# The output weights' bit conversion through a PSUM bank, and a new order of all steps

## The chip, the core and the metric

The program runs on one core of one Trainium2 chip. The metric is the device time of one execution in microseconds (us). Five engines work side by side: TensorE (PE, matmuls; PEld is its weight load), VectorE (DVE), ScalarE (ACT), GpSimd (POOL) and SyncE (SP), which here issues every DMA. PE, DVE and ACT write PSUM, a buffer of eight banks of 128 x 512 float32; all else lies in SBUF.

## What is computed

Three blocks follow each other on 8 batches of 576 rows of width 512. In short:

```python
# attention over pooled keys and values (8 heads of 64; pool of 8 along the sequence: 576 -> 72)
k_p, v_p = mean over 8 rows of k, v
x = softmax(q @ k_p.T / 8) @ v_p                      # (8, 576, 512)
# first MLP: 512 -> 1024 -> 512
h = relu(x @ w_in); c = conv over 3 neighbouring rows of h with conv_w
x = (h * sigmoid(c)) @ w_out                          # w_out: 1024 x 512
# second MLP with spatial gating
h = gelu(x @ w_in2); u, v = two halves of h; v = layernorm(v) * g_ln
out = x + (u * (w_sg @ v + b_sg)) @ w_out2            # w_out2: 512 x 512
```

Five inputs (`w_in`, `conv_w`, `w_out`, `w_in2`, `w_out2`) come as 64-bit floats, and the kernel turns them into float32 by bit operations.

## The kernel before

Matmuls run on operands that are split into a high part (rounded to the format fp32r) and a low remainder; a product is three matmuls, high x high, low x high and high x low.

**Tasks and steps.** Every piece of work is a generator. A step is what it issues between two `yield`s. A table of step keys, `ORDER`, names in one line of text which generator goes on next: a letter for the task, a number for its tile, and after the point the batch or chunk. Each instruction is pinned behind the one before it on its engine, so `ORDER` fixes the order on every engine, and that of SP's DMAs. The tasks that matter here:

- `k`, `v`, `q`/`p` load keys, values and queries; `K` makes the pooled, transposed keys `KBT` (for batch 1 by summing on PE, L106, then copies on ACT, L295/L296, and on DVE, L298/L301); `s` makes scores on PE (L419) and the softmax; `e` the transposed weights; `a` attention times values into `xh` and `xl`.
- `i` converts a piece of `w_in`, `t` a piece of `w_out` (8 of each), `l` a piece of `w_out2` (4).
- `I` is a tile of the first MLP's hidden layer: 12 matmuls into a bank `psi`, then relu and a tap on ACT (L558, L568), two taps on DVE (L570, L571), tanh on ACT (L573), and `g` on DVE (L577), which is the last reader of the bank. `O` multiplies by `w_out` into three banks `pso`; after the last tile ACT (L604) and DVE (L602) empty them.
- `y` loads the first MLP's result transposed, `T` makes the operands `xc` of the second MLP from it (subtractions on POOL, L694; high part on ACT, L699; low part on DVE or POOL, L134); `n` and `u` are its products (L747).
- `L`, `S`, `R` load and split the normalised half, `d` is the spatial product (L747, with evictions on DVE, L977, and the gate on POOL, L981), `D` splits the gated values, `o` multiplies by `w_out2` into a bank `psi` and stores.

**Banks.** PSUM's eight banks are three `psa`, two `psi` and three `pso`, each kind used in turn. A tile that asks for a bank waits for the last reader of the tile that had it before.

**A conversion.** `weight` loads 128 x 1024 words (512 KB), and `to_f32` makes 128 x 512 float32 of them by three DVE instructions: L146 writes an intermediate, L149 changes it in place, L152 writes `t`, a tile of the pool `work` with three buffers (tag `y`, shared with `g` and other short-lived tiles). ACT then rounds `t` to the high part and POOL (for `w_out2` DVE) subtracts. For `w_in` the intermediate lies in a bank `pso`; for `w_out` and `w_out2` it is `t` itself.

**Stages.** By the profile's time: attention of batch 0 and the first weights up to 63 us; attention of batch 1, the first tiles `I`/`O` and all of `t` up to 121 us; attention and first MLP together up to 554 us; second MLP's products up to 750 us; spatial product and output up to the end.

Of the kernel before, what the change touches and what calls it, by code (L numbers as in the profile page):

```python
# [26 lines left out]
def pooled_attention_gated_mlps(  # L27
# [24 lines left out]
    w_in, conv_w, w_out, w_in2, w_out2 = (a.bitcast(U32) for a in (w_in, conv_w, w_out, w_in2, w_out2))  # L52
    B, H, S, D = q.shape
# [26 lines left out]
    slot = ctx.enter_context(tc.tile_pool(name="slot", bufs=1))  # L80
# [27 lines left out]
    dve, pool = nc.vector, nc.gpsimd  # L108
    LO_IN = [pool for f in range(NF)]
    LO_OUT = [pool for f in range(NF)]  # L110
# [22 lines left out]
    def subtract(out, in0, hi, eng=nc.vector):  # L133
        eng.tensor_tensor(out=out, in0=in0, in1=hi.bitcast(F32), op=ALU.subtract)  # L134

    def to_f32(raw, t, tmp=None):

        w = raw.rearrange("p (n t) -> p t n", t=2)
        lo, up = w[:, 0, :], w[:, 1, :]
        ti = t.bitcast(U32)
        mi = ti if tmp is None else tmp.bitcast(U32)
        nc.vector.tensor_scalar(out=mi, in0=up, scalar1=3, scalar2=0x3FFFFFF8,  # L146
                                op0=ALU.logical_shift_left, op1=ALU.bitwise_and)
        yield
        nc.vector.scalar_tensor_tensor(out=mi, in0=up, scalar=0xC0000000, in1=mi,  # L149
                                       op0=ALU.bitwise_and, op1=ALU.bitwise_or)  # L150
        yield
        nc.vector.scalar_tensor_tensor(out=ti, in0=lo, scalar=29, in1=mi,  # L152
                                       op0=ALU.logical_shift_right, op1=ALU.bitwise_or)
        yield
# [43 lines left out]
    def weight(pool_, tag, src, eng, bank_, done):  # L198
        raw = pool_.tile([128, 1024], U32, tag=tag, name=f"{tag}raw")
        dst = raw  # L200
        if len(src.shape) == 3:
            dst = raw.rearrange("p (a b) -> p a b", a=src.shape[1])
        nc.sync.dma_start(out=dst, in_=src)
        yield
        t = work.tile([128, 512], F32, tag="y", name="t")
        yield from to_f32(raw, t, bank_() if bank_ else None)
        hl = pool_.tile([128, 2, 512], F32R, tag=tag, name=f"{tag}hl")
        done(hl)
        nc.scalar.copy(out=hl[:, 0, :], in_=t)
        yield  # L210
        subtract(hl[:, 1, :], t, hl[:, 0, :], eng)
# [11 lines left out]
    def t_w_out(f, *_):  # L223
        return weight(slot, f"w{f}", w_out[128 * f:128 * f + 128, :], LO_OUT[f], None,
                      lambda hl: wo.__setitem__(f, hl))
# [384 lines left out]
    w2 = {}  # L610
# [289 lines left out]
    wo2 = {}  # L900

    def t_w_out2(i, *_):
        p, tag = ((slot, "w4"), (slot, "w6"), (w2["q"], "T3"), (w2["q"], "T4"))[i]
        return weight(p, tag, w_out2[128 * i:128 * i + 128, :], dve, None, lambda hl: wo2.__setitem__(i, hl))
# [35 lines left out]
    g2 = {}  # L940
# [81 lines left out]
    def t_o2(i, b):  # L1022
# [14 lines left out]
        else:  # L1037
            for e in range(2):
                r0 = S * (b - 1 + e) + 128 * NM
                nc.sync.dma_start(out=out[r0:r0 + REM, :], in_=ob[REM * e:REM * e + REM])  # L1040


    tasks = {"z": t_setup, "c": t_coef, "i": t_w_in, "t": t_w_out, "k": t_k, "K": t_kfin, "v": t_v, "V": t_vfin,
             "q": t_q, "p": t_qtr, "s": t_s, "e": t_e, "x": t_x, "h": t_hg, "a": t_a, "I": t_i, "O": t_o, "A": t_att_close,
             "w": t_w2, "W": t_wsum, "Q": t_wsplit, "B": t_x2_open, "y": t_x2, "T": t_xc, "n": t_v2, "u": t_u,
             "g": t_sg, "G": t_sgsum, "H": t_sgsplit, "J": t_sgrest, "l": t_w_out2, "L": t_load, "S": t_sc, "R": t_vr,
             "b": t_bsg, "U": t_uload, "d": t_sp, "D": t_g, "m": t_res, "o": t_o2}
    running = {}
# [4 lines left out]
    def step(key):  # L1053

        if key not in running:
            i, _, b = key[1:].partition(".")
            running[key] = iter(tasks[key[0]](int(i or 0), int(b or 0)) or ())
        more = next(running[key], 0)
        issued = nc.cur_bb.bb.instructions
        for n in range(seen[0], len(issued)):  # L1060
            ins = issued[n]
            if ins.engine in last:
                tc.add_manual_dep(ins, last[ins.engine], pin, reason="order")
            last[ins.engine] = ins.name
        seen[0] = len(issued)
        return more is None

    for key in ORDER.split():
        step(key)
# [30 lines left out]
```

## Time and profile before

| | |
|---|---|
| median of 3 runs | 967.24 us (965.71 to 967.61) |
| the profiled execution's own time | 966.23 us |
| its span, first to last instruction | 964.3 us |
| mean granted clock of TensorE | 0.989 of full speed |
| busy PE / DVE / POOL / ACT | 923.4 / 776.4 / 562.8 / 529.3 us |

The span is what the views below show; 1.93 us of the execution's time lie around it. "Busy" of PE is not PE at its peak: a matmul that runs at half the clock is busy for longer. In a row of the timeline the first number is the start, the second the time until the end, and what stands in brackets is the engine's idle time before the row and what ended it.

### The profile page before, as it was taken

How to read it: one execution, taken by the hardware profiler on the slowest of the kernel's cores; microseconds unless marked ns; L12 is line 12 of the kernel's file. 1: busy time of each engine (PE TensorE's matmuls, PEld its weight loads, DVE VectorE, ACT ScalarE, POOL GpSimd, SP SyncE). 2: the span in 40 equal slices, each digit the busy share in tenths (PEclk: the TensorE clock that was granted, in tenths of full speed). 3: DMA queues.
4: the chain of work that ended last, by engine and by line, in shares of the span. 5: the costliest groups of instructions: out<-in, count | busy, mean ns of one | idle time of the engine just before them, and what ended most of it. 6: DMA issues, size and time to landing. Idle time of an engine off the chain costs nothing.

```text
span 964.3 us, 15821 instructions
## 1 busy us (share of the span) xinstructions
PE 923.4 (96%) x5396; PEld 844.2 (88%) x5396; DVE 776.4 (81%) x1399; ACT 529.3 (55%) x1108; POOL 562.8 (58%) x630
## 2 busy tenths in 40 slices
PE   5899999999999999999999989999999899999998
PEld 4787789899899998898998889999999788999996
DVE  5888997878889788797788478898887887887773
ACT  2756576667767666766557356655656323332221
POOL 3777797877868676356345257544563655554430
PEclk9899999999999999999999989999999999999999
DMA  9966174555747446232620674576536557476454
GB/s 241 243 190 164 45 186 118 131 148 155 158 129 145 129 126 138 60 104 69 157 70 22 123 150 119 156 204 171 146 140 217 179 156 259 142 219 180 159 179 131
DMA packets 182700, 143.61 MB, mean 149 GB/s; under 512 B 99776, under 2 KB 136924, under 8 KB 182620
## 3 DMA queue, kind: packets, MB, share of 16 engines
q1 hardware_dynamic: 182620, 142.61, 55.1%
q8 instruction: 42, 0.69, 0.3%
q14 instruction: 38, 0.31, 0.1%
HBM read 94.20 MB, written 48.37 MB: 148 GB/s over the span
## 4 chain that ended last, share of the span: by engine, by line
PE 75%; POOL 8%; DVE 8%; issue 3%; DMA 2%; ACT 2%; SPq 1%; POOLq 0%; DVEq 0%; ACTq 0%
PE psi L106 18%; PE psa L747 13%; PE pso L747 12%; PE pso L99 5%; PE pso L101 5%; PE pso L100 5%; PE psi L99 3%; PE psi L100 3%; PE psi L101 3%; PE psa L106 3%; PE psa L419 3%; POOL raw L251 1%; POOL xb L694 1%; POOL en L449 1%; DVE t L152 1%
## 5 line engine op out<-in xcount | busy, mean ns | idle before, releaser
L134 POOL TENSOR_TENSOR hg<-g,hg 128x384 fp32r<-128x384 f32 x96 | 100.3, 1053 | 74.2 <-ACT hg L580 68.0
L981 POOL TENSOR_TENSOR u<-u,tmp 128x288 f32<-128x288 f32 x64 | 60.6, 965 | 61.9 <-DVE tmp L977 41.6
L573 ACT ACTIVATE psi<-psi 128x384 f32<-128x384 f32 x96 | 45.7, 477 | 62.5 <-DVE psi L571 62.2
L694 POOL TENSOR_TENSOR xb<-xb 128x768 f32<-128x768 f32 x24 | 46.5, 1938 | 55.1 <-DVE xc L134 14.3
L570 DVE SCALAR_TENSOR_TENSOR psi<-h,coef,psi 128x384 f32<-128x384 f32 x96 | 58.7, 611 | 20.1 <-ACT psi L568 19.7
L558 ACT ACTIVATE h<-psi 128x386 f32<-128x386 f32 (+1 forms) x96 | 47.4, 493 | 43.5 <-PE psi L106 42.9
L617 ACT CAST sc<-vf 128x512 fp32r<-128x512 f32 x48 | 29.0, 620 | 72.6 <-POOL vf L928 42.2
L134 POOL TENSOR_TENSOR eTl<-xb,eTh 128x512 fp32r<-128x512 f32 (+1 forms) x30 | 46.4, 1545 | 32.9 <-ACT eTh L503 32.8
L577 DVE SCALAR_TENSOR_TENSOR g<-psi,h 128x384 f32<-128x384 f32 x96 | 52.5, 548 | 13.3 <-ACT psi L573 10.8
L571 DVE SCALAR_TENSOR_TENSOR psi<-h,coef,psi 128x384 f32<-128x384 f32 x96 | 59.8, 623 | 3.4
L419 PE MATMUL psa<-KBT,qT 128*128 128x144 f32 (+1 forms) x320 | 54.5, 300 | 7.5 <-DVE KBT L298 3.0
L419 PEld LDWEIGHTS psa<-KBT,qT 128*128 128x128 f32 (+1 forms) x320 | 45.6, 185 | 15.3 <-DVE KBT L298 3.3
L568 ACT ACTIVATE psi<-h,coef 128x384 f32<-128x384 f32 x96 | 56.3, 586 | 3.1
L747 PE MATMUL pso<-wc,xc 128*128 128x256 f32 x378 | 52.1, 286 | 6.0 <-ACT ob L604 2.9
L747 PEld LDWEIGHTS pso<-wc,xc 128*128 128x128 f32 x378 | 49.5, 192 | 7.4 <-ACT ob L604 3.3
L580 ACT CAST hg<-g 128x384 fp32r<-128x384 f32 x96 | 47.7, 507 | 14.3 <-DVE g L577 13.7
L747 PE MATMUL psa<-wc,xc 128*128 128x256 f32 x378 | 51.4, 283 | 1.1 <-ACT tmp L770 1.0
L747 PEld LDWEIGHTS psa<-wc,xc 128*128 128x128 f32 x378 | 49.0, 189 | 1.7 <-ACT tmp L770 1.4
L747 PE MATMUL psa<-xc,wc 128*128 128x384 f32 x252 | 49.7, 346 | 0.3 <-ACT tmp L814 0.2
L747 PE MATMUL pso<-xc,wc 128*128 128x384 f32 x252 | 49.1, 338 | 0.6 <-ACT tmp L814 0.6
L699 ACT CAST xc<-xb 128x768 fp32r<-128x768 f32 x42 | 34.6, 835 | 23.1 <-DVE xb L682 11.9
L457 POOL TENSOR_TENSOR en<-e,rs 128x512 f32<-128x512 f32 (+1 forms) x30 | 32.0, 1066 | 24.4 <-ACT hg L580 10.1
(396 smaller groups left out, 3120.2 us busy)
## 6 DMA issues: line engine op xcount, KB each, us to landing
xb<-eds SPq DMA_DIRECT2D x24, 384.0 KB, 3.4
x2s<-ob SPq DMA_DIRECT2D x36, 256.0 KB, 2.3
xb<-x2s SPq DMA_DIRECT2D x48, 192.0 KB, 4.1
us<-ub SPq DMA_DIRECT2D x24, 384.0 KB, 3.2
vs<-vg SPq DMA_DIRECT2D x18, 512.0 KB, 3.2
u<-us SPq DMA_DIRECT2D x16, 576.0 KB, 6.2
vf<-vs SPq DMA_DIRECT2D x16, 512.0 KB, 4.5
out_dram<-ob SPq DMA_DIRECT2D x32, 256.0 KB, 2.0
```

The source lines that it names most:

```text
L99: nc.tensor.matmul(out=out_, lhsT=ah, rhs=bh, start=first, stop=False)
L100: nc.tensor.matmul(out=out_, lhsT=al, rhs=bh, start=False, stop=False)
L101: nc.tensor.matmul(out=out_, lhsT=ah, rhs=bl, start=False, stop=last)
L106: nc.tensor.matmul(out=out_, lhsT=a, rhs=b_, start=(i == 0), stop=(i == n - 1))
L134: eng.tensor_tensor(out=out, in0=in0, in1=hi.bitcast(F32), op=ALU.subtract)
L419: nc.tensor.matmul(out=ps[0:n, 2 * SP * x:2 * SP * x + 2 * SP], lhsT=qT[:, p, 0:n], rhs=KBT[:, p, :], start=True, stop=True)
L568: nc.scalar.activation(out=y, in_=tap(1), func=AF.Copy, scale=cw(1, f))
L570: nc.vector.scalar_tensor_tensor(out=y, in0=tap(0), scalar=cw(0, f), in1=y, op0=ALU.mult, op1=ALU.add)
L571: nc.vector.scalar_tensor_tensor(out=y, in0=tap(2), scalar=cw(2, f), in1=y, op0=ALU.mult, op1=ALU.add)
L694: pool.tensor_tensor(out=x, in0=y, in1=z, op=ALU.subtract)
L747: nc.tensor.matmul(out=ps, lhsT=a, rhs=b_, start=first and i == 0, stop=last and i == n - 1, skip_group_check=True)
L981: pool.tensor_tensor(out=z, in0=z, in1=o, op=ALU.mult)
```

## The change

The two tasks give `weight` a bank of the kind `psi` for the intermediate, so that L146 and L149 write PSUM and only L152 writes SBUF. And `ORDER` is another line of text: the same 3617 steps, each as often as before, in a different sequence.

```diff
-ORDER = '''z k0.0 k1.0 k2.0 z z p0.0 c p1.0 p2.0 v0.0 v1.0 p3.0 ...'''
+ORDER = '''(the same keys in another sequence)'''
...
     def t_w_out(f, *_):
-        return weight(slot, f"w{f}", w_out[128 * f:128 * f + 128, :], LO_OUT[f], None,
+        return weight(slot, f"w{f}", w_out[128 * f:128 * f + 128, :], LO_OUT[f], i_bank,
                       lambda hl: wo.__setitem__(f, hl))
...
-        return weight(p, tag, w_out2[128 * i:128 * i + 128, :], dve, None, lambda hl: wo2.__setitem__(i, hl))
+        return weight(p, tag, w_out2[128 * i:128 * i + 128, :], dve, i_bank, lambda hl: wo2.__setitem__(i, hl))
```

DVE, around the first conversion of `w_out` (`w0raw`) and the pooled keys of batch 1 (`KBT`); `psi<-h,coef,psi` are the taps of the first tile `I`, `g` its end. Before:

```order
L146 TENSOR_SCALAR t<-w0raw 128x512
L149 SCALAR_TENSOR_TENSOR t<-w0raw,t 128x512
L152 SCALAR_TENSOR_TENSOR t<-w0raw,t 128x512
L570 SCALAR_TENSOR_TENSOR psi<-h,coef,psi 128x384
L571 SCALAR_TENSOR_TENSOR psi<-h,coef,psi 128x384
L298 COPY KBT<-psa 64x3x72
L301 COPY KBT<-psa 64x64
L146 TENSOR_SCALAR t<-w1raw 128x512
L149 SCALAR_TENSOR_TENSOR t<-w1raw,t 128x512
L577 SCALAR_TENSOR_TENSOR g<-psi,h 128x384
L152 SCALAR_TENSOR_TENSOR t<-w1raw,t 128x512
```

The same place now:

```order
L146 TENSOR_SCALAR psi<-w0raw 128x512
L149 SCALAR_TENSOR_TENSOR psi<-w0raw,psi 128x512
L570 SCALAR_TENSOR_TENSOR psi<-h,coef,psi 128x384
L571 SCALAR_TENSOR_TENSOR psi<-h,coef,psi 128x384
L152 SCALAR_TENSOR_TENSOR t<-w0raw,psi 128x512
L577 SCALAR_TENSOR_TENSOR g<-psi,h 128x384
L298 COPY KBT<-psa 64x3x72
L301 COPY KBT<-psa 64x64
L146 TENSOR_SCALAR psi<-w1raw 128x512
L149 SCALAR_TENSOR_TENSOR psi<-w1raw,psi 128x512
L152 SCALAR_TENSOR_TENSOR t<-w1raw,psi 128x512
```

The two conversions have no other work between their last instructions and the copies of `KBT`: the copies now stand behind `g`, and the second conversion is whole behind them.

PE at the same place: 40 sums of batch 1's keys (`ident,st`), the first tile `I` (`wi0hl`), transposes of queries (`ident,qb`, L397) and the scores (L419) that read `KBT`. Before:

```order
L106 MATMUL psa<-ident,st_174 64x128 x24
L106 MATMUL psi<-xh,wi0hl 128x386
...
L106 MATMUL psa<-ident,st_174 64x128 x8
L106 MATMUL psa<-ident,st_174 64x64 x8
L419 MATMUL psa<-KBT,qT 128x144 x2
L106 MATMUL psi<-xh,wi1hl 128x386
```

Now:

```order
L106 MATMUL psa<-ident,st_174 64x128 x16
L106 MATMUL psi<-xh,wi0hl 128x386
...
L106 MATMUL psa<-ident,st_174 64x128 x16
L106 MATMUL psa<-ident,st_174 64x64 x8
L397 MATMUL psa<-ident,qb 128x128 x4
L419 MATMUL psa<-KBT,qT 128x144 x4
L106 MATMUL psi<-xh,wi1hl 128x386
```

The tile `I` stands 8 sums further ahead, four transposes stand between the last sums and the scores, and both halves of the scores come before the next tile `I`.

ACT, where the first MLP ends and the second begins: `xc<-xb` are the high parts of the new operands (L699), `ob<-pso` empties the banks of the last `O`. Before:

```order
L580 CAST hg<-g 128x384 x2
L699 CAST xc<-xb 128x768 x4
L604 ACTIVATE ob<-pso 128x512
L699 CAST xc<-xb 128x768
L604 ACTIVATE ob<-pso 128x512
L699 CAST xc<-xb 128x768
```

Now:

```order
L580 CAST hg<-g 128x384 x3
L699 CAST xc<-xb 128x768 x2
L604 ACTIVATE ob<-pso 128x512 x2
L699 CAST xc<-xb 128x768 x4
```

Both evictions stand together behind the second operand, where they stood behind the fourth and the fifth.

## Rows read from the trace of the kernel before

**Rows 1.** Stages: length, busy (x) of PE, PEld, DVE, ACT, POOL; clock, DMA, GB/s.

```profile
15.00:63.00 48.00, 40.61 (x307) 34.86 (x306) 41.42 (x80) 28.68 (x73) 34.02 (x50) 0.93 1.07 262
63.00:140.00 77.00, 70.73 (x390) 61.37 (x389) 70.38 (x141) 49.66 (x108) 59.01 (x82) 0.98 0.49 116
140.00:554.00 414.00, 413.40 (x2190) 373.03 (x2188) 331.57 (x599) 270.32 (x539) 259.10 (x310) 1.00 0.47 118
554.00:566.00 12.00, 7.50 (x35) 7.06 (x34) 7.17 (x6) 6.19 (x10) 10.79 (x6) 0.72 0.72 124
566.00:750.00 184.00, 180.53 (x1253) 177.28 (x1252) 156.19 (x272) 113.15 (x236) 94.33 (x78) 1.00 0.57 165
750.00:776.00 26.00, 21.36 (x143) 20.11 (x142) 22.87 (x40) 9.07 (x19) 15.42 (x14) 0.93 0.66 213
776.00:964.30 188.30, 183.60 (x1070) 165.53 (x1069) 141.72 (x258) 49.03 (x119) 85.43 (x80) 1.00 0.56 174
```

**Rows 2.** PE's waits over the whole span: us in total, times, longest.

```profile
PE psa L397 <- DMA q<-in_q_dram: 8.4, 1, 8.4
PE psa L747 <- DVE tmp L977: 3.6, 2, 1.9
PE psi L106 <- DVE g L577: 0.9, 3, 0.5
```

**Rows 3.** DVE busy (x) on tile t alone: the eight conversions of `w_out`.

```profile
57.00:66.00 9.00, 5.74 (x6) 0.85 0.72 165
77.00:121.00 44.00, 11.96 (x18) 1.00 0.41 100
```

**Rows 4.** DVE busy (x) by L146 alone: the four conversions of `w_out2`.

```profile
640.00:653.00 13.00, 2.79 (x2) 1.00 0.61 213
764.00:774.00 10.00, 0.91 (x2) 0.83 0.54 148
```

**Rows 5.** The three lines by form: duration ns min/median/max, first and last start.

```profile
L146 DVE TENSOR_SCALAR psa<-w2raw x8: 682/687/689, 473.9 to 500.0; 128x512 uint32<-128x512 uint32 x8
L146 DVE TENSOR_SCALAR t<-w5raw x1: 419/419/419, 106.4 to 106.4; 128x512 uint32<-128x512 uint32 x1
L149 DVE SCALAR_TENSOR_TENSOR psa<-w2raw,psa x8: 685/688/696, 474.6 to 502.0; 128x512 uint32<-128x512 uint32 x8
L152 DVE SCALAR_TENSOR_TENSOR w2f<-w2raw,psa x8: 677/680/689, 478.8 to 506.7; 128x512 uint32<-128x512 uint32 x8
```

**Rows 6.** Timeline of DVE, ACT, PE and POOL around the first conversion.

```profile
55.81 1.30 POOL L134 TENSOR_TENSOR wi5hl<-t,wi5hl 128x512 fp32r<-128x512 f32 x1
57.15 1.24 DVE L146 TENSOR_SCALAR t<-w0raw 128x512 uint32<-128x512 uint32 x1 [1.02 <-POOL wi5hl L134]
59.16 1.63 DVE L152 SCALAR_TENSOR_TENSOR t<-w0raw,t 128x512 uint32<-128x512 uint32 x1
59.70 0.39 ACT L295 COPY KBT<-psa 64x288 f32<-64x288 f32 x1
62.01 0.38 DVE L298 COPY KBT<-psa 64x216 f32<-64x216 f32 x1
62.44 0.76 PE L419 MATMUL psa<-KBT,qT 128*128 128x144 f32 x4 [2.03 <-DVE KBT L298]
67.68 0.60 PE L397 MATMUL psa<-ident,qb 128*128 128x128 f32 x4
```

**Rows 7.** Timeline: a tile `I` (`wi3hl`) from its first matmul to its `g`.

```profile
72.40 0.42 PE L106 MATMUL psi<-xh,wi3hl 128*128 128x386 f32 x1
81.11 0.55 DVE L577 SCALAR_TENSOR_TENSOR g<-psi,h 128x384 f32<-128x384 f32 x1
```

**Rows 8.** Timeline of DVE and PE where the second MLP begins.

```profile
555.34 3.71 DVE L134 TENSOR_TENSOR xc<-xb,xc 128x768 fp32r<-128x768 f32 x2 [1.63 <-ACT xc L699]
557.16 0.97 PE L747 MATMUL pso<-wc,xc 128*128 128x256 f32 x6 [2.92 <-ACT ob L604]
559.71 1.65 PE L747 MATMUL pso<-wc,xc 128*128 128x256 f32 x6 [1.58 <-DVE ob L602]
```

2 lines of the change are left out of this document (1 added, 1 removed).

## The prediction

> **What bounds the kernel now.** I read the small table first: PE is busy for 923.4 of 964.3 us, so at most 41 us can come from PE's waits, and a little more from stretches at half the clock. The second view is the table of stages [rows 1]. From 140 to 554 us PE is busy for 413.40 of 414.00: nothing that DVE, ACT or POOL do there can be seen in the time as long as they keep up. The idle time of PE sits elsewhere: 7.4 us from 15 to 63 (48.00 - 40.61), 6.3 from 63 to 140, 4.5 from 554 to 566, 3.5 from 566 to 750, 4.6 from 750 to 776, and 8.4 at the very start, where the first queries are on their way [rows 2]. The granted clock is below 1 in the same stretches: 0.93 from 15 to 63, 0.72 from 554 to 566. DVE is the engine to look at next: from 15 to 140 it works for 41.42 + 70.38 = 111.8 of 125 us [rows 1], more than 89%, while PE does no more than 111.3. So in the first 140 us DVE and PE are about equally full, and an instruction that DVE is spared there can move PE. The third view, the timeline, shows where it does: PE sits idle for 2.03 us until 62.44 because DVE copies `KBT` at 62.01 only, and what stands before that copy on DVE is the first conversion of `w_out` [rows 6].
>
> **The bank instead of the tile.** What a conversion costs with its intermediate in PSUM stands in the trace, since `w_in2` is converted so eight times: medians of 687, 688 and 680 ns [rows 5], 2.06 us for the three. The eight conversions of `w_out` take 5.74 us (two, from 57 to 66) and 11.96 us (six, from 77 to 121) [rows 3]; with 2.06 each they would take 4.11 and 12.33. That is -1.63 and +0.37. The four of `w_out2` differ mainly in L146: 2.79 us for two and 0.91 for two [rows 4] against 1.37 for two, -1.42 and +0.46. Over all twelve DVE gets 2.2 us back, but only the first two conversions, where DVE is what PE waits for, make a term.
>
> The quick form is slower in PSUM: 419 ns for L146 where SBUF holds its output and POOL is out of the way, 687 in a bank [rows 5]; but with POOL at work the same SBUF form took 1.24 us, and L152 reading the tile took 1.63 [rows 6]. The Trainium skill says both: "VectorE: DVE Perf Modes", section "Why PSUM operands drop a tier", that a 32-bit operand in PSUM leaves the double rate, and "GPSIMD Engine Reference", section "8. Key points", that POOL shares its SBUF interfaces with such instructions of DVE. By the first alone twelve times 0.27 us would be lost on DVE, +3.2 in all; the sums measured here, quick and stretched forms together, decide for the second.
>
> There is a second effect at 57.15: L146 waited 1.02 us for POOL's `wi5hl` [rows 6], because `t` is one of three shared buffers and L146 already writes it. Now L146 and L149 write the bank, and only L152 asks for the buffer. DVE was free at 57.15 - 1.02 = 56.13; two instructions of 0.69 take it to 57.5, and `wi5hl` ends at 57.11, so the wait is covered.
>
> **The order at the first conversion.** PE now does the four transposes of queries (0.60 us, as its row at 67.68 shows [rows 6]) between the last key sums and the scores. They were ahead of the sums, so the sums end 0.60 earlier, at 62.44 - 2.03 - 0.60 = 59.81, and the transposes fill the time until 60.41. The copies then set the scores: ACT's two, of which the first takes 0.39, some 0.6; DVE's two, from 62.01 to the scores at 62.44, 0.5 [rows 6]. That gives 59.81 + 0.6 + 0.5 = 60.9, if DVE is free by 60.4. It is, although `g` stands ahead of the copies now: from 57.5 on it has two taps of about the length of `g`, 0.6 each, the last instruction of the conversion, 0.68, and `g`, 0.55 [rows 5, 7], and so ends at 59.9. So the scores start at 60.9, not 62.44: -1.5 us. Late next is ACT's first copy, which needs the sums themselves. Bounds: -2.03 (the whole wait) and +1.6. The upper one is a load: half of batch 1's keys is now issued behind two more weight pieces of 512 KB; at 262 GB/s [rows 1] 1 MB is 4.0 us, less the tile `I` (some 2.4 us) that PE does first.
>
> **From 63 to 140.** DVE starts this stretch about two us earlier, and its work in it is the same but for +0.37. PE has 6.3 us of idle time there, most of it ended by DVE. I take 1.0 of it as gained: -1.0, bounds -4 (most of what DVE ends) and +4 (the bank, see below). From 15 to 63 the order differs nearly everywhere, with the same instructions up to the last piece of `w_in`; the trace gives me no term there: 0, bounds -2 and +2.
>
> **Where the second MLP begins.** PE waited 2.92 us for an eviction on ACT and then 1.58 for one on DVE [rows 8]. Both evictions now come ahead of the operand splits behind which they stood, so the first product (0.97) moves up into the wait. The second still needs the low part of an operand on DVE, which ends at 555.34 + 3.71 = 559.05 and whose inputs did not change; PE then starts at 559.1 instead of 559.71. I take that: -0.6. Bounds 0 (POOL's next operands are the limit in any case) and -1.6 (the moved product counts as well).
>
> **The rest.** From 140 to 554 PE has no idle time to win, only some to lose: 0, bound +2. From 566 to 750 the conversions of `w_out2` give DVE 1.42 us, under a PE that idles 3.5 of 184 us: 0, bounds -1 and +1. From 764 on two conversions cost 0.46 more where PE waits for `tmp` on DVE (3.6 us in two waits [rows 2]), and the split of the next batch now stands ahead of some evictions; followed by hand from instruction to instruction PE reaches the same product at the same time within 0.3 us: +0.2, bounds -2 and +2. The tail from 776 keeps its last products and stores: 0.
>
> **Sum.** -1.5 - 1.0 - 0.6 + 0.2 = -2.9 us: 963.3 for the profiled execution of 966.23. The median of the three runs lies 1.01 above that one, so the median comes to 964.3.
>
> **The rivals.**
>
> *The banks become the wait (slower).* There are two banks `psi`. A tile `I` holds one from 72.40 to 81.66, 9.3 us [rows 7]. From 63 to 121 nine such tiles take 83 of the 116 us that two banks offer, and seven conversions now come in. As long as each holds its bank for under (116 - 83) / 7 = 4.7 us they fit; back to back they hold it for 2.06, but in the new order most are split by other instructions of DVE (a row of the softmax, a tap). From 4.7 on every tile behind one is late. PE waited for `g` of an earlier tile 0.9 us in three times, 0.5 at the longest [rows 2]. Seven times 0.5 is 3.5 us, seven times a whole conversion 14.4; nearer to the first I take 6, and 964.3 + 6 = 970.3. For it: no conversion took a bank `psi` before, so the rows show nothing of what a tile behind one waits. Against: tiles are spread thin in this stretch, since scores and attention stand between them.
>
> *Nothing to see.* DVE is spared 2.2 us of 776, PE's idle time only changes its place, and DMA, full from 15 to 63 (1.07 [rows 1]), or POOL set the pace of the first stage. Then the gain at 62.44 is lost again by 140: -0.6 + 0.2, some 966.8. For it: 59 of 77 us of POOL are busy as well from 63 to 140.
>
> *More than that.* If DVE's lead holds, PE loses less to the low clock too: 0.07 of 48 us and 0.02 of 77 are 3.4 and 1.5 us [rows 1]. With half of both and 2 us more of the idle time from 63 to 140 it would be 964.3 - 4.4, some 960.
>
> **How the numbers follow.** Forecast 0.52, own range 962.3 to 966.3; banks 0.20; nothing to see 0.20; more 0.08. A difference of 0.2%, 1.9 us, is about what can be told from none, so faster means under 965.3 and slower over 969.2. Faster: four fifths of the forecast, all of "more" and a little of the third, 0.52. Slower: the banks and the far bounds of the others, 0.23. Same: 0.25. The range that leaves out a tenth on each side runs from 959.5 to 970.3.
>
> **What would show it.** In the new profile: L146 and L149 on the twelve pieces near 687 ns each with no long one; no wait of L146 on POOL's `wi5hl`; the scores of batch 1 with 0.5 us of idle time before them, not 2.03; PE's idle time from 63 to 140 at 5 us or so; the first product of the second MLP without a wait for `ob` and the second at about 5 us behind the last `O`. I am wrong if PE waits for `g` or for L152 by more than 2 us in all (the banks), if PE idles as long as before from 55 to 140 us, or if a wait appears between 140 and 554.

## The result, and the profile after

The changed kernel took 957.08 us (955.07 to 958.37, 4 runs) beside 966.48 us for the kernel before on the same chip: a ratio of 0.9902, interval [0.9878, 0.9926]. A second series of six runs gave 955.74 us, 0.9909 [0.989, 0.9928]. So it is faster by 9 to 10 us. The forecast was 964.3 us with a range from 959.5 to 970.3: the sign is right, the size is not.

The stages of the changed kernel, in the columns of [rows 1]. From the fourth on they are shifted by the 5 us that the kernel is ahead at the end of the first MLP. At its end it is 11 us ahead, so the last three rows hold a little more or less work than the rows of before (1267 matmuls for 1253, 157 for 143, 1044 for 1070):

```profile
0.00:15.00 15.00, 6.54 (x30) 5.46 (x31) 6.57 (x13) 3.50 (x7) 4.70 (x15) 1.00 0.99 211
15.00:63.00 48.00, 41.43 (x320) 36.38 (x320) 41.99 (x83) 30.16 (x76) 35.13 (x52) 0.96 1.10 264
63.00:140.00 77.00, 72.04 (x401) 61.81 (x400) 71.04 (x143) 51.75 (x113) 58.40 (x84) 1.00 0.54 127
140.00:549.00 409.00, 407.13 (x2159) 367.99 (x2158) 324.37 (x590) 266.98 (x533) 254.93 (x304) 1.00 0.48 117
549.00:561.00 12.00, 7.30 (x32) 6.54 (x31) 7.91 (x7) 5.20 (x8) 9.89 (x6) 0.72 0.74 151
561.00:745.00 184.00, 182.12 (x1267) 179.11 (x1267) 155.30 (x277) 114.31 (x236) 94.40 (x80) 1.00 0.59 169
745.00:771.00 26.00, 23.67 (x157) 21.80 (x156) 25.26 (x47) 10.34 (x23) 16.55 (x15) 1.00 0.67 219
771.00:953.00 182.00, 177.66 (x1044) 160.76 (x1042) 130.26 (x245) 47.46 (x116) 82.59 (x78) 1.00 0.55 174
```

Length less busy PE is PE's idle time, and (1 - clock) times length is what the low clock costs a busy PE. Idle time falls from 9.3 to 8.5 us in the first row (PE is busy for 5.66 of its 15 us in the kernel before), 7.4 to 6.6 in the second, 6.3 to 5.0 in the third, 3.5 to 1.9 in the sixth and 4.6 to 2.3 in the seventh; it rises from 0.6 to 1.9 in the fourth; the fifth keeps 4.5 and has 4.7. The clock gives back 1.4 us in the second row (0.93 to 0.96), 1.5 in the third, 1.8 in the seventh. The gain thus lies ahead of 140 us and behind 561 us, and nearly half of it is clock.

Part of it is there ahead of the wait that the prediction followed. These two rows end where PE begins to wait for the scores of batch 1, in the kernel before and in the changed one; PE has run the same number of matmuls (324) by then, 2.1 us sooner in the changed kernel:

```profile
0.00:60.41 60.41, 45.71 (x324) 39.23 (x324) 44.00 (x83) 31.41 (x78) 36.15 (x62) 0.94 1.08 256
0.00:58.30 58.30, 44.20 (x324) 38.06 (x324) 44.10 (x86) 31.52 (x77) 35.50 (x61) 0.97 1.08 251
```

PE's waits, as in [rows 2] (us in total, times, longest):

```profile
PE psa L397 <- DMA q<-in_q_dram: 8.3, 1, 8.3
PE pso L747 <- ACT xc L699: 2.5, 1, 2.5
PE pso L747 <- DVE tmp L977: 2.2, 1, 2.2
PE pso L747 <- DVE xc L134: 2.0, 1, 2.0
PE psi L106 <- DVE g L577: 1.1, 3, 0.5
PE psa L419 <- DVE KBT L298: 0.9, 1, 0.9
```

The waits for `ob` at the second MLP's start [rows 8] are gone, and two for `xc` stand in their place, 2.46 + 2.04 against 2.92 + 1.58 us:

```profile
552.23 0.38 PE L747 MATMUL pso<-wc,xc 128*128 128x256 f32 x1 [2.46 <-ACT xc L699]
554.65 1.44 PE L747 MATMUL pso<-wc,xc 128*128 128x256 f32 x5 [2.04 <-DVE xc L134]
```

The wait for `g`, which the rival of the banks named, has hardly grown: 1.1 us in three for 0.9.

The conversions in the bank (form, duration ns min/median/max, first and last start; L146 of the other pieces takes 673 to 695 ns as well, and L149 666 to 697):

```profile
L146 DVE TENSOR_SCALAR psi<-w4raw x2: 674/684/695, 94.4 to 645.2; 128x512 uint32<-128x512 uint32 x2
L146 DVE TENSOR_SCALAR psi<-w6raw x2: 673/681/689, 111.3 to 636.2; 128x512 uint32<-128x512 uint32 x2
L146 DVE TENSOR_SCALAR psi<-T4raw x1: 677/677/677, 756.9 to 756.9; 128x512 uint32<-128x512 uint32 x1
```

### The profile page after: what moved, and what is told of

Its sections match the earlier page's. It is cut to its first block, busy times and chain, and to the rows that moved or that the text cites. A ratio compares the mean times of both kernels' runs of the same rounds, so it can differ in the third digit from the quotient of the medians.

```text
span 953.3 us, 15822 instructions
## 1 busy us (share of the span) xinstructions
PE 917.9 (96%) x5396; PEld 839.9 (88%) x5396; DVE 762.7 (80%) x1399; ACT 529.7 (56%) x1108; POOL 556.6 (58%) x630
## 4 chain that ended last, share of the span: by engine, by line
PE 77%; DVE 9%; DMA 5%; POOL 3%; ACT 3%; SPq 2%; issue 1%; DVEq 0%; POOLq 0%; ACTq 0%
PE psi L106 17%; PE pso L747 14%; PE psa L747 13%; PE pso L99 6%; PE pso L101 6%; PE pso L100 6%; PE psi L99 3%; PE psi L100 3%; PE psi L101 3%; PE psa L106 3%; PE psa L419 3%; DMA qb<-in_q_dram 1%; DVE psi L570 1%; DMA st<-in_k_dram 1%; DVE psi L571 1%
## 5 line engine op out<-in xcount | busy, mean ns | idle before, releaser
L981 POOL TENSOR_TENSOR u<-u,tmp 128x288 f32<-128x288 f32 x64 | 61.4, 980 | 50.8 <-DVE tmp L977 33.9
L694 POOL TENSOR_TENSOR xb<-xb 128x768 f32<-128x768 f32 x24 | 45.4, 1892 | 51.8 <-DVE xc L134 26.5
L419 PE MATMUL psa<-KBT,qT 128*128 128x144 f32 (+1 forms) x320 | 52.0, 295 | 2.5 <-DVE KBT L298 0.9
L419 PEld LDWEIGHTS psa<-KBT,qT 128*128 128x128 f32 (+1 forms) x320 | 44.5, 183 | 8.9 <-issue 2.7
L503 ACT CAST eTh<-xb 128x768 fp32r<-128x768 f32 (+1 forms) x30 | 41.0, 1366 | 9.1 <-DVE xb L499 8.9
L747 PEld LDWEIGHTS psa<-xc,wc 128*128 128x128 f32 x252 | 44.3, 195 | 1.7 <-POOL xc L134 0.8
```

The costliest lines, as they stand in the source:

```text
L419: nc.tensor.matmul(out=ps[0:n, 2 * SP * x:2 * SP * x + 2 * SP], lhsT=qT[:, p, 0:n], rhs=KBT[:, p, :], start=True, stop=True)
L747: nc.tensor.matmul(out=ps, lhsT=a, rhs=b_, start=first and i == 0, stop=last and i == n - 1, skip_group_check=True)
L981: pool.tensor_tensor(out=z, in0=z, in1=o, op=ALU.mult)
```

## The experiments

All ratios are against the kernel before, which ran beside each group with medians of 965.8 to 966.2 us. "Old" and "new" are the two orders; "first" and "second" bank stand for the conversions of `w_out` and of `w_out2`. In the old order with the bank, three of the eight pieces of `w_out` (1, 4 and 7) keep the tile, as the edit shows; all eight in the old order were not run.

**The two halves of the change, each alone.**

```diff
 # e1: the old ORDER
-... LO_OUT[f], None,
+... LO_OUT[f], i_bank if f in (0, 2, 3, 5, 6) else None,
-... dve, None, lambda
+... dve, i_bank, lambda
 # e2: the new ORDER, None and None
```

> The bank without the new order: the order of the steps is that of the kernel before, word for word; five of the eight conversions of the first output weight (numbers 0, 2, 3, 5, 6) and all four of the second take their two bit operations through the bank, the other three (1, 4, 7) keep the SBUF tile. Theory A (the order makes the gain, the bank next to nothing): 966.5 us like the kernel before, within 1.5 us; the stretch 750 to 776 keeps its idle time of about 4.5 us and its half clock. Theory B (the bank makes it, since a conversion no longer waits for a free tile behind other work and VectorE gets away from GpSimd): 959 to 962 us. Theory C (the bank costs, the order pays for it): 968 to 971 us, with TensorE waiting for g (L577) or L152 before input projections.

> The new order without the bank: the order of the steps is that of the changed kernel, all conversions keep the SBUF tile. Theory A: 957 us like the changed kernel, within 1.5 us. Theory B: 964 to 967 us. Theory C (the bank costs a little): 954 to 956 us. If the bank is what lets the new order run (a conversion placed early finds no free tile), the loss shows at the first conversions: the first L146 on wi5hl or its like again waits a microsecond or more, and TensorE idles over 1.5 us ahead of the scores of batch 1.

Measured: the bank in the old order 969.6 us, 1.0037 [1.0024, 1.005]; the new order without the bank 971.6 us, 1.0063 [1.0044, 1.0082]. Each half makes the kernel slower, both together make it 1% faster. Theory C is right for the first run, and none of the three for the second: it lost more than any of them allowed. The sign that its expectation named for a fourth case, the bank as what lets the new order run, is there (below: a wait of 1.54 us before the first L146, and 3.72 us of idle time ahead of the scores).

The bank in the old order, timeline around 75 us:

```profile
75.44 0.68 DVE L146 TENSOR_SCALAR psi<-w2raw 128x512 uint32<-128x512 uint32 x1
78.12 0.67 DVE L149 SCALAR_TENSOR_TENSOR psi<-w2raw,psi 128x512 uint32<-128x512 uint32 x1
79.16 0.68 DVE L152 SCALAR_TENSOR_TENSOR t<-w2raw,psi 128x512 uint32<-128x512 uint32 x1
79.30 0.69 PE L106 MATMUL psi<-xh,wi4hl 128*128 128x386 f32 x1 [4.70 <-DVE g L577]
```

The old order spreads conversion 2 from 75.44 to 79.84; it holds one of the two banks, the tile `I` ahead of it the other until its `g` is through, and the next tile `I` waits 4.70 us. This is the rival of the banks, in the place and by the mechanism that the prediction gave; the new order puts the steps so that it doesn't happen.

The new order without the bank, timeline around the first conversion, to be read against [rows 6]; then the changed kernel at the same place:

```profile
56.89 1.47 DVE L146 TENSOR_SCALAR t<-w0raw 128x512 uint32<-128x512 uint32 x1 [1.54 <-POOL wi5hl L134]
58.40 1.10 DVE L149 SCALAR_TENSOR_TENSOR t<-w0raw,t 128x512 uint32<-128x512 uint32 x1
60.60 1.10 DVE L152 SCALAR_TENSOR_TENSOR t<-w0raw,t 128x512 uint32<-128x512 uint32 x1
62.62 1.81 PE L419 MATMUL psa<-KBT,qT 128*128 128x144 f32 x6 [3.72 <-DVE KBT L298]
```

```profile
54.99 0.69 DVE L146 TENSOR_SCALAR psi<-w0raw 128x512 uint32<-128x512 uint32 x1
55.71 0.69 DVE L149 SCALAR_TENSOR_TENSOR psi<-w0raw,psi 128x512 uint32<-128x512 uint32 x1
57.50 0.68 DVE L152 SCALAR_TENSOR_TENSOR t<-w0raw,psi 128x512 uint32<-128x512 uint32 x1
59.23 1.00 PE L419 MATMUL psa<-KBT,qT 128*128 128x144 f32 x6 [0.93 <-DVE KBT L298]
```

The new order sets conversions beside POOL's work. With the tile the three instructions then take 1.47 + 1.10 + 1.10 us, behind a wait of 1.54, and the scores stand 3.72 us; with the bank they take 0.64 to 0.70 each wherever they stand. It is the same with later ones: without the bank L149 on `w6raw` took 2.07 and 2.22 us, the second time beside POOL's L694:

```profile
646.00 3.82 POOL L694 TENSOR_TENSOR xb<-xb 128x768 f32<-128x768 f32 x2 [8.53 <-DVE xc L134]
648.15 2.22 DVE L149 SCALAR_TENSOR_TENSOR t<-w6raw,t 128x512 uint32<-128x512 uint32 x1
```

**Where the two orders differ in worth.**

```diff
 # e3: new ORDER up to the step O7.11, the rest in the old one; bank in all twelve
 # e4: old ORDER up to O7.11, the rest in the new one; banks as in e1
```

> The new order up to the last output product of the first MLP (the step O7.11), the old order of the steps from there on; all conversions through the bank. By the two traces the changed kernel ends that product 4.0 us earlier (549.8 against 553.8 us) and gains the other 7.0 us after it. Theory D (each part gains by its own order): 966.5 - 4.0 = 962.5 us, and idle time and half clock at 750 to 776 us as in the kernel before. Theory E (what follows runs better only because the first part left it a better start): 957 to 959 us.

> The old order up to the last output product of the first MLP, the new order of the steps from there on; the first output weight's conversions 0, 2, 3, 5, 6 and all of the second's through the bank. Theory D: 966.5 - 7.0 = 959.5 us. Theory E: 964 to 967 us. If the gain behind 554 us is the second weight's bank and not the order, the kernel with the bank and the old order gains it too, 959 to 961 us.

Measured: 962.3 us, 0.9962 [0.9948, 0.9975], and 964.6 us, 0.9987 [0.9978, 0.9997]. The first is what theory D said, except that its trace lacks the half clock near 770 us. The second is not: its number is theory E's (964 to 967). But both theories were priced against the wrong kernel: up to 554 us this run is the bank in the old order (969.6), and against that it gains 5.0 us, where theory E has next to no gain and theory D 7.0. Set against the changed kernel (957.1), the run with the old second part loses 5.2. So the order behind the first MLP is worth 5 us by two pairs, and the part ahead of it, with its bank, some 4 against the kernel before.

**Which bank, and what it is about the bank.**

```diff
 # e5: new ORDER, i_bank and None        # e6: new ORDER, None and i_bank
 # e7: the changed kernel, but
+    def ob_tile():
+        return outp.tile([128, 2, 512], F32, tag="ob", name="tb")[:, 0, :]
-... LO_OUT[f], i_bank,
+... LO_OUT[f], ob_tile if f < 2 else i_bank,
 # e8: e1 without conversion 2
-... i_bank if f in (0, 2, 3, 5, 6) else None,
+... i_bank if f in (0, 3, 5, 6) else None,
```

> The new order, the bank for the eight conversions of the first output weight alone; the four of the second weight keep the SBUF tile. The new order without any bank took 971.6 us, and its last output product of the first MLP ended at 560.6 us where the changed kernel's ended at 549.1: 11.5 us lie before that point and about 4.6 us behind it. Theory F (each bank mends its own stretch, and what is won early is kept): 957.1 + 4.6 = about 961.5 us. Theory G (only the first conversions matter; what comes later is hidden): 957 to 958.5 us. VectorE's bit operations of the second weight beside GpSimd would show 1.1 to 2.1 us each instead of 0.69.

> The new order, the bank for the four conversions of the second output weight alone; the eight of the first keep the SBUF tile. Theory F: 957.1 + 11 = about 968 us, with the wait of about 3.7 us ahead of the scores of batch 1 and lost clock near 61 to 68 us. Theory G: 970 to 972 us.

> The changed kernel, but conversions 0 and 1 of the first output weight put their two bit operations into an SBUF tile of their own (half of a tile that the output products use later and that is free at 55 to 62 us) in place of the bank. It tells a place of its own (nothing to wait for) from PSUM (nothing to share with GpSimd). Theory H (it is the place: the rotating tile comes free late): the first L146 doesn't wait 1.55 us and its operations take 0.7 us, the scores of batch 1 wait 0.9 us as in the changed kernel, 957 us. Theory I (it is the memory: VectorE's SBUF-to-SBUF operations beside GpSimd are slow): no wait of 1.55 us, but L146, L149 and L152 of conversion 0 take 1.1 to 1.5 us each, the scores wait 2 to 2.5 us, 958 to 962 us with the clock that may go with it.

> The old order; the bank for conversions 0, 3, 5, 6 of the first output weight and all of the second: the run with the bank in the old order less conversion 2. There TensorE stood 4.70 us before an input projection (I4.0) whose bank conversion 2 held, with half clock soon after (77.6 to 84.5 us), and 969.6 us in all. Theory J (that one held bank makes the loss): 969.6 - 4.3 = 965 us, and 963 to 964 where the clock stays up too. Theory K (the bank in the old order loses little by little at many places): 968 to 969.5 us.

Measured: first bank only 963.3 us, 0.9966 [0.9951, 0.998]; second only 967.3, 1.0013 [0.9999, 1.0027]; own SBUF tile 961.0, 0.9959 [0.9942, 0.9976]; old order less conversion 2 964.6, 0.9983 [0.9974, 0.9991]. Theory F holds within 2 us: each bank mends its own stretch. Theory J holds: without the one held bank the old order is no longer slower than before but 1.6 us faster, and the scores of batch 1 wait 0.83 us there instead of 2.03:

```profile
62.51 0.76 PE L419 MATMUL psa<-KBT,qT 128*128 128x144 f32 x4 [0.83 <-DVE KBT L298]
```

So the bank shortens this wait without a new order. What that is worth in time isn't shown apart: in this trace the scores start no earlier than before (62.51 for 62.44 us), since PE came to the wait 1.3 us later, and the 1.6 us are those of eight conversions in the bank.

The first conversion in an SBUF tile of its own (lines stand three further down in that kernel). The profiled execution was a long one, 969.0 us, with a wait of 2.71 us for a load at 35 us; only the durations are read:

```profile
56.94 3.09 DVE L149 TENSOR_SCALAR tb<-w0raw 128x512 uint32<-128x512 uint32 x1
60.06 1.10 DVE L152 SCALAR_TENSOR_TENSOR tb<-w0raw,tb 128x512 uint32<-128x512 uint32 x1
62.25 1.10 DVE L155 SCALAR_TENSOR_TENSOR t<-w0raw,tb 128x512 uint32<-128x512 uint32 x1
```

The wait for `wi5hl` is gone, and nothing is won by it: the instruction starts at once and takes 3.09 us beside POOL, and the scores wait 3.80 us in this trace. So it is the memory and not the place (theory I, though one of the three instructions and the wait of the scores are longer than it said).

**Behind the first MLP.** First the changed kernel with the old end, and the kernel before with the new end; then, each on the kernel before, the second bank alone and the new order from O7.11 to 735 us alone.

```diff
 # e9:  new ORDER up to 735 us, the rest in the old one; bank in all twelve
 # e10: old ORDER up to 735 us, the rest in the new one; second bank
 # e14: old ORDER; second bank
 # e15: old ORDER up to O7.11, new up to 735 us, old to the end; second bank
```

> The changed kernel up to about 735 us (the u products of the last but one group), the old order of the steps from there on, all conversions through the bank. It tells how much of what the changed kernel gains behind the first MLP (some 5 us) lies in the order of the spatial products' start, where the kernel before idled 4.6 us and the changed one 2.3 us. Theory L (there it lies): 957.1 + 2.3 = 959.5 us, up to 961 if the clock drops there too, and TensorE again waits for tmp (L977) at three or four places before 780 us. Theory M (it lies in the u and n products from 566 to 735 us, which wait 3.5 us before and 1.9 us after): 957 to 958 us.

> The kernel before up to about 735 us, the new order from there on; the first output weight keeps the SBUF tile, the four conversions of the second take the bank. The smallest part of the change that holds the start of the spatial products. Theory L: 966.2 - 2.3 = 964 us, down to 962.3 where the half clock near 770 us goes too. Theory M: 966 us.

> The kernel before, the bank for the four conversions of the second output weight and nothing else. Theory P (in the old order the second bank is worth nothing, since no conversion there waits or stands beside GpSimd for long): 966.2 us, within 1 us, waits at 750 to 776 us as before. Theory Q (the second bank alone made the 3.6 us of the run with the old order up to 735 us): 962.5 us.

> The old order up to the last output product of the first MLP, the new one from there to 735 us, the old one again to the end; the bank for the second weight alone. Theory R (the stretch 566 to 735 us gains by its own order with the bank: there the runs of the new order took 169.3 us from the tenth product of u0.0 to d0.0, those of the old 173.3): 966.2 - 3 to 4 = 962 to 963 us. Theory S (it gains only behind the new first part): 965 to 966 us.

Measured: 957.4 us, 0.9915 [0.9902, 0.9928]; 962.6, 0.997 [0.9958, 0.9982]; 965.8, 0.9999 [0.999, 1.0007]; 962.8, 0.9971 [0.9961, 0.9981]. The second bank alone is worth nothing (theory P). With it the new order of the stretch from 554 to 735 us gives the kernel before 3.1 us (theory R), that of the end 3.2 (theory L). In that stretch the new order needs the bank: PE's waits in the row from 566 to 750 us, shifted with each kernel, come to 3.3 us in the kernel before, with or without the second bank, to 1.8 in the changed kernel, and to 4.3 in the new order with the first bank only. The first run fits theory M by its time, yet its trace has the waits of theory L; PE's waits for `tmp` of 0.5 us and more in the kernel before, then in this run, then in the changed kernel:

```profile
756.78 1.06 PE L747 MATMUL pso<-sgp,sc 128*128 128x288 f32 x6 [0.61 <-DVE tmp L977]
761.91 1.06 PE L747 MATMUL psa<-sgc,sc 128*128 128x288 f32 x6 [1.67 <-DVE tmp L977]
768.33 1.97 PE L747 MATMUL psa<-sgc,sc 128*128 128x288 f32 x12 [1.90 <-DVE tmp L977]
```

```profile
748.95 1.07 PE L747 MATMUL pso<-sgp,sc 128*128 128x288 f32 x6 [0.61 <-DVE tmp L977]
753.04 1.06 PE L747 MATMUL psa<-sgc,sc 128*128 128x288 f32 x6 [0.64 <-DVE tmp L977]
759.28 1.84 PE L747 MATMUL psa<-sgc,sc 128*128 128x288 f32 x12 [1.71 <-DVE tmp L977]
764.08 1.86 PE L747 MATMUL pso<-sgc,sc 128*128 128x288 f32 x12 [1.64 <-DVE tmp L977]
```

```profile
751.75 1.07 PE L747 MATMUL pso<-sgp,sc 128*128 128x288 f32 x6 [2.25 <-DVE tmp L977]
```

Why the new end needs the bank is seen where it has none, in the run with the first bank only:

```profile
764.56 1.00 DVE L146 TENSOR_SCALAR t<-T3raw 128x512 uint32<-128x512 uint32 x1 [2.29 <-POOL u L981]
766.09 0.51 DVE L977 SCALAR_TENSOR_TENSOR tmp<-psa,coef,bsg 128x288 f32<-128x288 f32 x1
766.74 1.54 PE L747 MATMUL psa<-sgc,sc 128*128 128x288 f32 x5 [2.97 <-ACT g L996]
```

The new order has both conversions under way at once, with the L146 of each ahead of this L977. The second L146 asks for one more buffer of the pool that `t` shares with other short-lived tiles, and waits for POOL's L981 to be done; DVE stands for 2.29 us with L977 behind it, and PE for 2.97. The view names ACT's L996 as what ended PE's wait. But L977 ends at 766.60, only 0.14 us before PE starts, and in the changed kernel the same product starts at 759.79, ahead of the same casts of L996 (760.48), so it doesn't wait for them. In the bank the same L146 runs at 757.94 and L977 at 759.13, and neither DVE nor PE waits.

**The clock, and the wait that is left.**

```diff
 # e11: the kernel before, ahead of the first scores of batch 1
+            for x in range(8 if (t, b, a) == (0, 1, 0) else 0):
+                nc.tensor.matmul(out=ps[:, 0:128], lhsT=ident, rhs=ident, start=True, stop=True)
 # e12: the changed kernel, sixteen of these into Z ahead of mm(Z, 5, True) of the step n0.0
 # e13: the changed kernel;  e16: the changed kernel, in its ORDER
-R0.1 d1.0 d1.0
+d1.0 d1.0 R0.1
```

> The kernel before with one addition: eight products of the identity with itself (their results are overwritten by the scores) fill the wait of TensorE of 2.03 us ahead of the scores of batch 1. Nothing else can start earlier by it. Theory N (the idle time is what lowers the clock behind it): no half clock at 63 to 67 us, 966.2 - 1.7 = 964.5 us. Theory O (the clock falls there for another reason): half clock as before, 966.2 to 967 us.

> The changed kernel with one addition: sixteen products of the identity with itself (overwritten by the real ones) ahead of the second product of the second MLP, where TensorE idled 2.46 and then 2.04 us waiting for xc, with half clock from 552.9 to 559.8 us. Theory N: the half clock goes, 957.1 - 3.4 = 953.7 us, less if the products of the identity run into the real one's inputs. Theory O: 957 to 958 us.

> The changed kernel again, for a second trace and more times. What belongs to the order repeats: TensorE waits 0.9 to 1.1 us ahead of the scores of batch 1, half clock absent at 63 to 67 us, one wait of about 2.2 us between 745 and 776 us. What belongs to one execution's clock may move: the half clock near 34 us (3.4 us long in the first trace) and near 553 us (6.9 us). 956 to 958 us.

> The changed kernel with one step later: VectorE's subtraction for vr of batch 1 (L134, 1.69 us at 749.03 us beside GpSimd) goes behind the two L977 of d1.0 that TensorE waited 2.25 us for. If that wait is on the path, 957.1 - 1.3 = 955.8 us, with a wait of about 1 us there; if what follows is late anyway, 957 us.

Measured: 966.1 us, 1.0001 [0.9992, 1.0009]; 957.2, 0.9904 [0.9892, 0.9917]; 955.7, 0.9909 [0.989, 0.9928]; 957.5, 0.9916 [0.99, 0.9933]. Stages of the kernel before, and the same two of the kernel with the filled wait:

```profile
57.00:63.00 6.00, 3.97 (x40) 3.40 (x38) 5.68 (x8) 2.55 (x6) 5.19 (x7) 1.00 0.78 164
63.00:67.00 4.00, 4.00 (x17) 4.00 (x16) 2.92 (x6) 1.75 (x4) 0.67 (x3) 0.57 0.48 133
```

```profile
57.00:63.00 6.00, 6.00 (x55) 5.50 (x54) 5.07 (x7) 2.96 (x7) 5.19 (x5) 1.00 0.90 195
63.00:67.00 4.00, 4.00 (x29) 3.97 (x29) 3.81 (x9) 2.06 (x5) 1.19 (x4) 1.00 0.48 137
```

With the wait filled the clock stays at 1.00 where it had been at 0.57: theory N is right about the cause at this place. It is wrong about the time, which is theory O's. The filling ran 0.7 us too long (the scores start at 63.16 instead of 62.44); where the other 1.0 us of the 1.7 went stays open, since that trace has its other stretches at half clock (near 36, 561 and 770 us) where the kernel before has them. The filling of the second MLP's start gave theory O's time as well; it only moved the low clock there: 0.52 from 553 to 560 us became 1.00, and 0.76 from 560 to 567, behind a new wait of 2.01 us for `tmp`.

The changed kernel's second trace repeats what belongs to the order: the scores wait 0.49 us (less than the 0.9 to 1.1 expected), the clock is 1.00 from 63 to 140, and the stretch from 745 to 771 has less idle time still:

```profile
58.95 1.25 PE L419 MATMUL psa<-KBT,qT 128*128 128x144 f32 x8 [0.49 <-DVE KBT L298]
63.00:140.00 77.00, 72.11 (x400) 61.86 (x399) 71.05 (x143) 51.82 (x112) 58.32 (x84) 1.00 0.54 127
745.00:771.00 26.00, 24.25 (x159) 22.30 (x158) 24.54 (x48) 10.49 (x23) 17.65 (x16) 1.00 0.69 219
```

The one wait left there (2.25 us in the first trace, 1.31 in the second) is not worth mending by the step that was moved: it falls to 0.61 us, and PE waits 1.30 a few products on.

```profile
750.87 1.06 PE L747 MATMUL pso<-sgp,sc 128*128 128x288 f32 x6 [0.61 <-DVE tmp L977]
754.54 1.06 PE L747 MATMUL psa<-sgc,sc 128*128 128x288 f32 x6 [1.30 <-DVE tmp L977]
```

No version that was run beats the changed kernel by more than its runs spread.

## Why the prediction was right in sign and too small

Step by step, as the prediction put it:

- **The scores of batch 1, -1.5.** Right for the wait. It fell from 2.03 [rows 6] to 0.93 and 0.49 us in the two traces (0.5 was forecast), and the bank does it, in the old order too. Not in the sum: the half clock behind that wait goes with it, 0.43 x 4 = 1.7 us more.
- **From 15 to 63, 0, bounds 2 each way.** Too small, by all of its bound. The scores start at 59.23 and 58.95 us, not at the 60.9 of the prediction, because PE comes to their wait 2.1 and 1.9 us sooner with the same number of matmuls (324) done. The new order without the bank comes 1.5 us sooner, so the order does most of this; no run takes its steps apart.
- **From 63 to 140, -1.0.** Right for the idle time: 6.3 to 5.0 and 4.9 us.
- **The second MLP's start, -0.6.** Wrong by the whole of it: the waits for `ob` are gone as forecast, but the second product starts at 552.23 and gets its low part at 554.65 only, for the splits themselves became the wait. Idle time there is 4.7 and 4.3 us, for 4.5 before.
- **From 566 to 750, 0, bounds 1 each way.** The first failed step. Idle time fell by 1.6 us, and the old kernel given the order from 554 to 735 us (with the second bank) gained 3.1; in its trace the idle time of this row fell by 2.1, and the clock from 554 to 566 was 0.86 for 0.72. The prediction asked here only what DVE is spared. But in the kernel before all 3.3 us of PE's waits in this row end on ACT (`tmp`, L770 and L814), and the new order moved those.
- **From 764 on, +0.2, bounds 2 each way.** The second failed step, and the larger. Idle time of the 26 us fell by 2.3 and 2.9, the old kernel given this end gained 3.2. The prediction followed the order by hand to one product, which it doesn't name, and found it at the same time; the first of these waits did stay, and grew (0.61 to 2.25 and 1.31 us). The waits behind it were not followed, and the prediction counted only two of them, 3.6 us, where the kernel before has five, 4.7 us: in the kernel before, two splits on DVE stand between those L977 (at 758.89 and 763.08 us, 1.33 and 1.23 us long); in the changed kernel both are through ahead of them (at 746.80 and 749.03), and the later waits don't come (one of 0.44 us in the second trace). With the second of the two put back among them, in the run with the moved step, a wait of 1.30 us is there again.
- **From 140 to 554, 0 (bound +2).** It cost 1.3 us of idle time, within the bound; a wait in this stretch was one of the signs of being wrong that the prediction named.
- **The rival of the banks.** Not in this kernel, but real: 4.70 us in the old order. With that stall taken out the run gained 5 us, near the 6 that the prediction set.
- **The rival "more than that", 960.** Nearest by its number, but not by its working: it took 2 us more of the idle time from 63 to 140, which fell by 1.3 and 1.4 in all, and put no gain behind 554 us.

So what was mis-sized is the order, from 554 us on above all: the prediction priced it at -0.4 in all and it is worth 5. Ahead of 554 us the price was -2.5, and some -4 was measured. The reason is in how the two halves were costed. The prediction asked what the bank saves in the places where the conversions stood, and found 2.2 us of DVE. But in the old order the tile costs little time where the conversions stand: there the second bank is worth 0.0 us, and eight conversions in the bank 1.6. What the bank buys is that a conversion may stand anywhere, beside POOL and in turn with another one, and the new order uses that: without the bank it takes 971.6 us, with it 957.1. A change of two parts was summed as if each had a price of its own, and the price is in the pair.

The clock is the other part. In the profiled execution it gave back about 5 of 11 us. Of these the 1.4 us from 15 to 63 are not in the second trace, whose clock there is 0.93 as before. The 1.7 us behind the scores repeat in every trace of the new order with the first bank. The half clock near 770 us, which is in the kernel before and not in the changed one, is absent too from all six traces that have the old end with the second bank, and that bank alone changed no time (in its trace PE idles 5.4 us from 750 to 776, for 4.6 before, so that waits took the place of the half clock); so it stays open how much of that is the change's. Open as well is why the old end costs the kernel before 3.2 us and the changed one 0.3 to 1.7: the waits are there in both. So is why 3.1 and 3.2, the gains of its two parts on the kernel before, come to more than the 5 of the whole. The one trace of the changed kernel with the old end had a mean clock of 0.997, against 0.994 and 0.992 in the two of the changed kernel. That can hide part of its waits in that execution, but doesn't explain why the median is as low.

## What to carry to other kernels

When a change frees an instruction (of a buffer, of another engine's work beside it) and moves it at once, price the pair: ask where the old order could not have put it, not what it saves where it stood. Follow a new order by hand through the whole stretch in which PE waits, not to the first product that comes out even, for the waits behind it are other instructions. And where a wait of PE goes, look at the granted clock of the few us behind it: here the half clock behind a wait of 2.03 us came to 1.7 us, though filling that wait alone changed no time.

## What the runs showed of the hardware

- An SBUF instruction of DVE next to POOL's work is slowed by much more than the prediction's rows showed: across the runs L146 on a 128x512 tile in SBUF took 0.40 (POOL idle when it began) to 3.09 us and L149 0.64 to 2.22, while both took 0.67 to 0.70 in the changed kernel, in the bank. That one operand in PSUM is enough was not expected: L146 and L149 still read the raw words from SBUF, and L152 still writes SBUF. The Trainium skill ("GPSIMD Engine Reference", section "8. Key points") says that POOL shares its SBUF interfaces with DVE's instructions of two SBUF inputs or a two-port mode; by that rule an operand in PSUM frees L149 and L152 of it, and the runs agree: 1.10 us each for the first conversion in SBUF, 0.69 and 0.68 in the bank.
- A wait of 2.03 us ahead of the scores of batch 1 was followed by 3.4 us at half clock (1.2 instead of 2.4 GHz). At this place the traces agree: in all seven with a wait of 2.03 to 4.31 us half clock follows, in none of the ten with 0.24 to 1.12 us, and not where the wait was filled. It is no rule for every place: behind the wait of 2.25 us at 751.75 the clock stayed at 1.00. And other stretches at half clock differ between executions of the same order of steps: between 29 and 38 us some 3 us in the first trace of the changed kernel, some 7 in the second and none in that with the old end; from 552 us on some 7, 7 and 3 us. So one trace doesn't tell what a change does to them.
